# Two weight chunks a slice with alternating operations in the first tile of a windowed-attention and PReLU-FFN kernel

## The chip, the cores and the metric

One core of one Trainium2 chip runs the kernel. The metric is the device time in microseconds (us) of one execution; lower is better. Before the change three runs took 962.49, 964.57 and 964.89 us (median 964.57).

## The reference

Attention with a window (heads 0 to 3: the last 32 keys; heads 4 to 7: every fourth of the last 128 keys), and then a feed-forward layer with a PReLU on its output:

```python
B, H, S, D = 8, 8, 576, 64
scores = scale * np.matmul(q, k.transpose(0, 1, 3, 2))
scores = np.where(masks[None], scores, -1e9)
attn = np.exp(scores - scores.max(-1, keepdims=True))
attn = attn / (attn.sum(-1, keepdims=True) + 1e-9)
x = np.matmul(attn, v).astype(np.float32).transpose(0, 2, 1, 3).reshape(B * S, H * D)  # 4608 x 512
h = x @ w_in                                         # float64 weights, 512 x 2048
g = np.maximum(h, 0.0) + alpha * np.minimum(h, 0.0)
out = (g @ w_out).astype(np.float32)                 # float64 weights, 2048 x 512
```

The weights and alpha come as float64, q, k and v as float32.

## The kernel before

**Attention.** The eight heads of a batch are four pairs, and `Pair(b, c)` handles one pair. Its steps: `load_qk`, `load_v` (DMA), `scores` (72 small matmuls into two PSUM tiles), `maxima` (VectorE: twelve masked reductions of 64 columns, six for each of the two PSUM tiles), `exponentials(a, z)` (ScalarE, ten in all), `divisions` (VectorE, four operations), `transposes` (TensorE), `copies` (ScalarE), `values` (72 small matmuls), `highs` (ScalarE) and `lows` (VectorE). The last two split the attention's result into a high and a low part of a reduced fp32 format, which are the tile `x` of the feed-forward layer.

**Feed-forward.** Rows of x are taken in nine tiles of 512, and the 2048 hidden columns in sixteen slices of 128. A product is three matmul passes: high by high, high by low, low by high. For slice n: `ffn_h` (12 matmuls), `ffn_relu` (ScalarE: relu of -h and of h), `ffn_sum` (VectorE), `ffn_high` (ScalarE: g's high part), `ffn_low` (VectorE: g's low part), `ffn_y` (12 matmuls; the first needs the high part alone, the rest the low part too). Later tiles use `ffn_parts`, two VectorE operations, in place of relu and sum.

**Weights.** Both matrices are 32 chunks of 128 x 512 float64 numbers (512 KB each), loaded by `load_weight` in the order of the list `wq`. A `Conversion` makes two fp32 parts of a chunk: `magnitude` (ScalarE, the absolute value of the upper words), `words` (VectorE, four operations that each need the one before: clamp, shift, sign, lower bits), `high` (ScalarE) and `low` (VectorE). This is done only in the prologue (one chunk for each of five pairs) and the first tile.

**Order.** On TensorE, VectorE, ScalarE and SyncE the order is that of the code; each engine runs its own instructions strictly in that order, and waits come from the tiles' uses. Loads are issued by SyncE (SP). Tiles with tag `g` (staged chunks and g) share five buffers, and so do those with tag `m` (magnitudes and the relu's results): a load waits until an earlier tile's last reader is done. The prologue is the loop over `s`, in which pair s is normalised while pair s-1 is multiplied by v and pair s+1 is scored. In the first tile (`begin`, n below 16) the slices do weights and attention together: slices 2, 6, 10 and 14 score a pair, the slice after holds its `exponentials(3)` and the `highs` and `lows` of the pair before (`held`), the next its `divisions`, the next its `transposes` and `copies`.

Of the kernel before, what the change touches and what calls it, by code (L numbers as in the profile page):

```python
# [50 lines left out]
def tile_window_attention_prelu_ffn(  # L51
# [47 lines left out]
    class Pair:  # L99
# [36 lines left out]

        def maxima(self):

            self.nm = sml.tile([P, NR], F32, tag="nm", name=f"nm_{self.id}")
            for e in range(2):  # L140
                for g in range(NG + 2):
                    rows = slice(0, P) if g < NG else slice(e * BQ, (e + 1) * BQ)
                    r = e * NG + g if g < NG else 2 * NG + g - NG
                    kind = self.kinds[g] if g < NG else 1
                    nc.vector.tensor_tensor_reduce(  # L145
                        out=self.pr[rows, r, :], in0=self.ps[e][rows, g, :], in1=mask_sb[rows, kind, :],
                        scale=-SCALE, scalar=3.0e38, op0=ALU.add, op1=ALU.min, accum_out=self.nm[rows, r:r + 1],
                    )

        def exponentials(self, a=0, z=NR):  # L150
# [92 lines left out]
    class Conversion:  # L243
# [12 lines left out]
        def words(self):  # L256
            a, af = self.a, self.a.bitcast(F32)
            lo, hi = self.st[:, :, 0], self.st[:, :, 1]
            nc.vector.tensor_scalar(out=af, in0=af, scalar1=F64_LOW, scalar2=F64_HIGH, op0=ALU.max, op1=ALU.min)  # L259
            nc.vector.tensor_scalar(  # L260
                out=a, in0=a, scalar1=3, scalar2=0x3FFFFFFF, op0=ALU.logical_shift_left, op1=ALU.bitwise_and)
            nc.vector.scalar_tensor_tensor(  # L262
                out=a, in0=hi, scalar=0xC0000000, in1=a, op0=ALU.bitwise_and, op1=ALU.bitwise_or)
            nc.vector.scalar_tensor_tensor(  # L264
                out=a, in0=lo, scalar=29, in1=a, op0=ALU.logical_shift_right, op1=ALU.bitwise_or)

# [113 lines left out]
    for s in range(NC):  # L380
        u = pairs[s]
        if s:
            pairs[s - 1].copies()
            pairs[s - 1].values()
# [3 lines left out]
        pairs[s + 1].load_v()  # L388
        u.maxima()
        u.exponentials()  # L390
        w.words()
        load()
        if s:
            pairs[s - 1].highs()
            pairs[s - 1].lows()
        w.high()
        u.divisions()
        u.transposes()
        w.low()
# [3 lines left out]
    u.values()  # L403
    v.maxima()
    u.highs()
    v.exponentials(0, 5)
    u.lows()
    ffn_h(0, 0)
    w.words()
    load()  # L410
    w.high()
    v.exponentials(5)
    v.divisions()
# [9 lines left out]

    late, w1 = w, conversion()
    pending, held = [], None
    for n in range(NTILE * NF):
# [6 lines left out]
        if begin:  # L433

            ffn_sum(t, f)
            ffn_high(t, f)
            if late:
                late.low()
            w2 = conversion()
            if w1:  # L440
                w1.words()
                w1.high()
                load()
            if n + 1 < NF:
                ffn_relu(t, f + 1)
            ffn_low(t, f)
            if w1:
                w1.low()
            if n in behind_at:
                behind_at[n].exponentials(3)  # L450
            if held:
                held.highs()
                held.lows()
                held = None
            if divided:
                divided.divisions()
            if w2:
                w2.words()
                w2.high()
                load()  # L460
            pending.append((t, f))
# [25 lines left out]
        if scored:  # L487
            if not begin:
                scored.exponentials(5)
            scored.load_v()  # L490
        if begin:
            late, w1 = w2, conversion()
        if n + 1 == NF:
# [61 lines left out]
```

## Time and profile before

| | us |
|---|---|
| median of three runs | 964.57 |
| the profiled execution | 961.82 |
| its span on the core | 960.0 |
| TensorE matmuls busy | 906.3 (94%) |
| VectorE busy | 528.5 (55%) |
| ScalarE busy | 308.0 (32%) |

The profiled execution is 2.75 us below the median of the runs, which spread over 2.4 us. In rows of the profile PE is TensorE, DVE VectorE, ACT ScalarE, SP SyncE; a row of a timeline has the start in us from the beginning of the span, the duration in us, engine, line, operation, output and input tiles with shapes, and in brackets the engine's idle time ahead of it and who ended it. Two starts that lie less than a duration apart mean that the engine overlaps the end of one operation with the next. In rows of stages there stand, for each engine, busy us and the number of instructions, then the granted TensorE clock, the DMA share and GB/s.

### The profile page before, as it was taken

Reading aid. Unit: us, or ns where it says so; the run is one execution under the profiler, and the core shown is the slowest. Engines: PE = TensorE matmul, PEld = TensorE weight load, DVE = VectorE, ACT = ScalarE, POOL = GpSimd, SP = SyncE. Lnnn points to the kernel's source line nnn. Section 1 sums busy time; section 2 is a strip of 40 time slices with the busy share of each in tenths; the row PEclk is TensorE's granted clock in tenths of the full one; section 3 lists DMA queues with packets and bytes.
Section 4 is the critical chain, followed back from the end, with each engine's and each line's share of the span. In section 5 each row is a group of like instructions: output and inputs, shape, how many; then the busy total and the mean of one; then the engine's idle time right before and its main releaser. Section 6 shows DMA issues by size and latency. Waiting matters only on the chain.

```text
span 960.0 us, 19918 instructions
## 1 busy us (share of the span) xinstructions
PE 906.3 (94%) x8224; PEld 741.8 (77%) x8224; DVE 528.5 (55%) x1607; ACT 308.0 (32%) x1075; POOL 0.7 (0%) x6
## 2 busy tenths in 40 slices
PE   4777876999999999999999999999999999999998
PEld 4655655778888888888888888888888888888886
DVE  6798798575555554545555455455555544334342
ACT  5655555432333232322232223223322311111111
POOL 0000000000000000000000000000000000000000
PEclk9988988999999999999999999999999999999999
DMA  7544533031112111211121112111211000001001
GB/s 260 193 134 159 156 121 110 36 109 51 51 51 94 50 51 51 86 42 39 39 88 49 50 51 94 51 51 51 80 65 51 26 12 33 1 1 44 1 1 44
DMA packets 30139, 65.39 MB, mean 68 GB/s; under 512 B 2784, under 2 KB 11104, under 8 KB 30048
## 3 DMA queue, kind: packets, MB, share of 16 engines
q1 hardware_dynamic: 30048, 64.11, 19.5%
q8 instruction: 65, 1.06, 0.4%
q14 instruction: 26, 0.21, 0.1%
HBM read 54.67 MB, written 9.44 MB: 67 GB/s over the span
## 4 chain that ended last, share of the span: by engine, by line
PE 83%; DVE 9%; ACT 5%; issue 1%; DMA 1%; SPq 0%; ACTq 0%
PE y L325 39%; PE h L284 36%; PE o L191 3%; PE s L122 3%; ACT pr L153 2%; PE t L173 2%; DVE wa L262 2%; DVE wa L264 2%; DVE wa L260 1%; DMA q<-qT 1%; DVE wa L259 1%; DVE x L229 1%; ACT early L153 1%; DVE wo L271 1%; ACT x L225 1%
## 5 line engine op out<-in xcount | busy, mean ns | idle before, releaser
L325 PE MATMUL y<-g,wo 128*128 128x512 f32 x1728 | 430.6, 398 | 26.8 <-DVE g L317 15.7
L284 PE MATMUL h<-x,wi 128*128 128x512 f32 x1728 | 422.5, 393 | 0.3 <-DVE x L229 0.2
L325 PEld LDWEIGHTS y<-g,wo 128*128 128x128 f32 x1728 | 327.5, 191 | 100.7 <-DVE g L317 20.3
L284 PEld LDWEIGHTS h<-x,wi 128*128 128x128 f32 x1728 | 324.2, 189 | 70.2 <-DVE x L229 2.3
L312 ACT CAST g<-m 128x512 fp32r<-128x512 f32 x144 | 89.4, 621 | 521.1 <-DVE m L307 516.2
L306 DVE TENSOR_SCALAR m<-h,al 128x512 f32<-128x512 f32 x128 | 96.1, 751 | 263.9 <-PE h L284 263.0
L317 DVE TENSOR_TENSOR g<-m,g 128x512 fp32r<-128x512 f32 x144 | 99.2, 689 | 77.4 <-ACT g L312 77.4
L153 ACT ACTIVATE pr<-pr,nm 128x64 f32<-128x64 f32 x300 | 100.3, 337 | 43.3 <-DVE nm L145 43.3
L307 DVE SCALAR_TENSOR_TENSOR m<-h,m 128x512 f32<-128x512 f32 x128 | 88.5, 691 | 4.4
L145 DVE CUSTOM_DVE_ANT_0 pr<-s,mask_sb 128x64 f32<-128x64 f32 x360 | 56.3, 213 | 25.9 <-PE s L122 25.0
L153 ACT ACTIVATION_READ_ACCUMULATOR pr<-pr,nm 128x1 f32 x300 | 56.8, 189 | 0.0
L229 DVE TENSOR_TENSOR x<-o,x 128x288 fp32r<-128x288 f32 (+8 forms) x112 | 36.0, 385 | 29.5 <-ACT x L225 29.5
L122 PEld LDWEIGHTS s<-k,q 64*32 64x32 f32 x2304 | 28.6, 111 | 21.0 <-DMA q<-qT 6.3
L122 PE MATMUL s<-k,q 64*32 64x64 f32 x2304 | 34.0, 237 | 11.0 <-DMA q<-qT 11.0
L191 PE MATMUL o<-pt,v 64*64 64x32 f32 x2088 | 38.7, 223 | 3.7 <-DVE nm L145 3.6
L191 PEld LDWEIGHTS o<-pt,v 64*64 64x64 f32 x2088 | 35.1, 137 | 7.3 <-issue 3.9
L225 ACT CAST x<-o 128x288 fp32r<-128x288 f32 (+8 forms) x112 | 30.4, 384 | 4.8 <-PE o L191 4.8
L145 DVE DVE_READ_ACCUMULATOR2_ANT nm<- 128x1 f32 (+1 forms) x384 | 28.8, 75 | 0.0
L163 DVE TENSOR_TENSOR pr<-pr,rs 128x512 f32<-128x512 f32 (+1 forms) x60 | 26.6, 484 | 1.0
L173 PE MATMUL t<-ident,pr 128*128 128x128 f32 x150 | 22.6, 284 | 3.6 <-DVE pr L163 3.6
L173 PEld LDWEIGHTS t<-ident,pr 128*128 128x128 f32 x150 | 18.7, 145 | 8.2 <-ACT wa L254 2.2
L180 ACT COPY pt<-t 128x320 f32<-128x320 f32 x64 | 22.6, 398 | 7.2 <-PE t L173 7.0
(35 smaller groups left out, 237.0 us busy)
## 6 DMA issues: line engine op xcount, KB each, us to landing
v<-vW SPq DMA_DIRECT2D x29, 576.0 KB, 3.8
k<-kT SPq DMA_DIRECT2D x32, 288.0 KB, 4.2
q<-qT SPq DMA_DIRECT2D x32, 288.0 KB, 4.4
out<-ob SPq DMA_DIRECT2D x36, 256.0 KB, 2.3
ws<-w_in SPq DMA_DIRECT2D x16, 512.0 KB, 4.0
ws<-w_out SPq DMA_DIRECT2D x16, 512.0 KB, 3.9
early<-vW SPq DMA_DIRECT2D x3, 576.0 KB, 6.8
mask_sb<-masks SPq DMA_DIRECT2D x1, 128.0 KB, 4.4
```

The lines of the kernel that those rows point to most:

```text
L122: nc.tensor.matmul(self.ps[e][col * BQ:(col + 1) * BQ, g, :], lhsT=self.q[rows, j * BQ:(j + 1) * BQ], rhs=self.k[rows, first_key(j):first_ ...
L145: nc.vector.tensor_tensor_reduce(out=self.pr[rows, r, :], in0=self.ps[e][rows, g, :], in1=mask_sb[rows, kind, :], scale=-SCALE, scalar=3.0 ...
L153: nc.scalar.activation(out=self.pr[rows, r, :], in_=self.pr[rows, r, :], func=AF.Exp, bias=self.nm[rows, r:r + 1], scale=-1.0, accum_out=s ...
L173: nc.tensor.transpose(out=self.tp[e][:, g, :], in_=self.pr[:, r:r + 2, :].rearrange("q h k -> q (h k)"), identity=ident)
L191: nc.tensor.matmul(self.po[u][e * D:(e + 1) * D, j, :], lhsT=self.v[rows, e, j, :], rhs=pt[:, :BQ], start=True, stop=True,)
L229: nc.vector.tensor_tensor(out=lo, in0=src, in1=hi.bitcast(F32), op=ALU.subtract)
L284: nc.tensor.matmul(ps, lhsT=wi[:, a, f, c, :], rhs=x[:, c, e, :], start=(n == 0), stop=(n == 3 * NC - 1))
L306: nc.vector.tensor_scalar(out=m, in0=ps, scalar1=0.0, scalar2=al[:, f:f + 1], op0=ALU.min, op1=ALU.mult)
L307: nc.vector.scalar_tensor_tensor(out=m, in0=ps, scalar=0.0, in1=m, op0=ALU.max, op1=ALU.add)
L312: nc.scalar.copy(out=g[:, 0, :], in_=ms[t, f])
L317: nc.vector.tensor_tensor(out=g[:, 1, :], in0=ms.pop((t, f)), in1=g[:, 0, :].bitcast(F32), op=ALU.subtract)
L325: nc.tensor.matmul(ys[t][c], lhsT=wo[:, a, f, c * P:(c + 1) * P], rhs=g[:, e, :], start=(f == 0 and n == 0), stop=(f == NF - 1 and n == 2),)
```

## The change

Four things are changed, all ahead of the second tile. In the prologue the four `words` operations of a chunk stand between the maxima of the second PSUM tile, copies and values of the pair before come behind four of the ten exponentials, divisions and transposes come ahead of the `highs` and `lows` of the pair before, and `load()` stands further ahead. In the first tile a slice takes its two chunks together: their `words` alternate, half of them ahead of `ffn_low` and half behind it. The two `magnitude` steps of the next slice stand at the end of a slice, and the two `high` steps of a slice's chunks at the start of the next one. And `held.highs()` and `held.lows()` stand ahead of `exponentials(3)`. No instruction is added or removed.

```diff
--- before.py
+++ after.py
@@ -134,8 +134,9 @@
                     for e in range(2):
                         self.score(e, NG + g, e, HB * g + HB - 1)
 
-        def maxima(self):
-
+        def maxima(self, between=()):
+
+            between = list(between)
             self.nm = sml.tile([P, NR], F32, tag="nm", name=f"nm_{self.id}")
             for e in range(2):
                 for g in range(NG + 2):
@@ -146,6 +147,8 @@
                         out=self.pr[rows, r, :], in0=self.ps[e][rows, g, :], in1=mask_sb[rows, kind, :],
                         scale=-SCALE, scalar=3.0e38, op0=ALU.add, op1=ALU.min, accum_out=self.nm[rows, r:r + 1],
                     )
+                    if e and between:
+                        between.pop(0)()
 
         def exponentials(self, a=0, z=NR):
             for r in range(a, z):
@@ -256,13 +259,16 @@
         def words(self):
             a, af = self.a, self.a.bitcast(F32)
             lo, hi = self.st[:, :, 0], self.st[:, :, 1]
-            nc.vector.tensor_scalar(out=af, in0=af, scalar1=F64_LOW, scalar2=F64_HIGH, op0=ALU.max, op1=ALU.min)
-            nc.vector.tensor_scalar(
-                out=a, in0=a, scalar1=3, scalar2=0x3FFFFFFF, op0=ALU.logical_shift_left, op1=ALU.bitwise_and)
-            nc.vector.scalar_tensor_tensor(
-                out=a, in0=hi, scalar=0xC0000000, in1=a, op0=ALU.bitwise_and, op1=ALU.bitwise_or)
-            nc.vector.scalar_tensor_tensor(
-                out=a, in0=lo, scalar=29, in1=a, op0=ALU.logical_shift_right, op1=ALU.bitwise_or)
+            return [
+                lambda: nc.vector.tensor_scalar(
+                    out=af, in0=af, scalar1=F64_LOW, scalar2=F64_HIGH, op0=ALU.max, op1=ALU.min),
+                lambda: nc.vector.tensor_scalar(
+                    out=a, in0=a, scalar1=3, scalar2=0x3FFFFFFF, op0=ALU.logical_shift_left, op1=ALU.bitwise_and),
+                lambda: nc.vector.scalar_tensor_tensor(
+                    out=a, in0=hi, scalar=0xC0000000, in1=a, op0=ALU.bitwise_and, op1=ALU.bitwise_or),
+                lambda: nc.vector.scalar_tensor_tensor(
+                    out=a, in0=lo, scalar=29, in1=a, op0=ALU.logical_shift_right, op1=ALU.bitwise_or),
+            ]
 
         def high(self):
             nc.scalar.copy(out=self.dst[:, 0, :], in_=self.a.bitcast(F32))
@@ -379,6 +385,9 @@
     load()
     for s in range(NC):
         u = pairs[s]
+        u.maxima(w.words())
+        u.exponentials(0, 4)
+        load()
         if s:
             pairs[s - 1].copies()
             pairs[s - 1].values()
@@ -386,30 +395,26 @@
         if s + 2 <= NC:
             pairs[s + 2].load_qk()
         pairs[s + 1].load_v()
-        u.maxima()
-        u.exponentials()
-        w.words()
-        load()
+        u.exponentials(4)
+        u.divisions()
+        u.transposes()
         if s:
             pairs[s - 1].highs()
             pairs[s - 1].lows()
         w.high()
-        u.divisions()
-        u.transposes()
         w.low()
         w = conversion()
     u, v = pairs[NC - 1], pairs[NC]
     u.copies()
     u.values()
-    v.maxima()
+    v.maxima(w.words())
+    load()
+    v.exponentials(0, 4)
     u.highs()
-    v.exponentials(0, 5)
     u.lows()
     ffn_h(0, 0)
-    w.words()
-    load()
+    v.exponentials(4)
     w.high()
-    v.exponentials(5)
     v.divisions()
     ffn_relu(0, 0)
 
@@ -421,7 +426,8 @@
     divide_at = {n + (2 if n < NF else 1): u for n, u in score_at.items() if n >= 0}
     turn_at = {n + (3 if 0 <= n < NF else 2): u for n, u in score_at.items()}
 
-    late, w1 = w, conversion()
+    late, now = [w], [conversion(), conversion()]
+    late[0].high = lambda: None
     pending, held = [], None
     for n in range(NTILE * NF):
         t, f = divmod(n, NF)
@@ -432,32 +438,39 @@
             ffn_h(*divmod(n + 1, NF))
         if begin:
 
+
+            a = late[0] if late else None
+            z = late[1] if len(late) > 1 else None
+            words = [op for ops in zip(*(w.words() for w in now)) for op in ops]
+            if a:
+                a.high()
             ffn_sum(t, f)
             ffn_high(t, f)
-            if late:
-                late.low()
-            w2 = conversion()
-            if w1:
-                w1.words()
-                w1.high()
+            if z:
+                z.high()
+            if a:
+                a.low()
+            half = len(words) // 2
+            for op in words[:half]:
+                op()
+            ffn_low(t, f)
+            if z:
+                z.low()
+            for op in words[half:]:
+                op()
+            for _ in now:
                 load()
             if n + 1 < NF:
                 ffn_relu(t, f + 1)
-            ffn_low(t, f)
-            if w1:
-                w1.low()
-            if n in behind_at:
-                behind_at[n].exponentials(3)
             if held:
                 held.highs()
                 held.lows()
                 held = None
+            if n in behind_at:
+                behind_at[n].exponentials(3)
             if divided:
                 divided.divisions()
-            if w2:
-                w2.words()
-                w2.high()
-                load()
+            late, now = now, [w for w in (conversion(), conversion()) if w]
             pending.append((t, f))
         elif n + 1 < NTILE * NF:
             ffn_parts(*divmod(n + 1, NF))
@@ -488,8 +501,6 @@
             if not begin:
                 scored.exponentials(5)
             scored.load_v()
-        if begin:
-            late, w1 = w2, conversion()
         if n + 1 == NF:
             ffn_parts(1, 0)
             ffn_high(1, 0)
```

VectorE in slice 4, before: `wa` are the magnitudes that become words (`wa1_5` is chunk 5 of w_out), `ws` the staged chunks, `wo` and `wi` the finished weights (their row is a `low`), `m` and `g` those of slice 4, `pr` and `rs` the tiles of `divisions`.

```order
L299 SCALAR_TENSOR_TENSOR m_0_4_1047<-m_0_4_1047,nal_82,h_0_4_1021 128x512
L271 TENSOR_TENSOR wo_90<-wa1_5_1038,wo_90 128x512
L259 TENSOR_SCALAR wa0_7_1085<-wa0_7_1085 128x512
L260 TENSOR_SCALAR wa0_7_1085<-wa0_7_1085 128x512
L262 SCALAR_TENSOR_TENSOR wa0_7_1085<-ws0_7_911,wa0_7_1085 128x512
L264 SCALAR_TENSOR_TENSOR wa0_7_1085<-ws0_7_911,wa0_7_1085 128x512
L317 TENSOR_TENSOR g_0_4_1105<-m_0_4_1047,g_0_4_1105 128x512
L271 TENSOR_TENSOR wi_89<-wa0_7_1085,wi_89 128x512
L160 TENSOR_SCALAR rs_1_1_1122<-sums1_85 128x10
L161 RECIPROCAL rs_1_1_1122<-rs_1_1_1122 128x10
L163 TENSOR_TENSOR pr0_83<-pr0_83,rs_1_1_1122 128x512
L163 TENSOR_TENSOR pr0_83<-pr0_83,rs_1_1_1122 64x128
```

After, the same slice:

```order
L305 SCALAR_TENSOR_TENSOR m_0_4_1053<-m_0_4_1053,nal_82,h_0_4_1020 128x512
L277 TENSOR_TENSOR wi_89<-wa0_6_910,wi_89 128x512
L263 TENSOR_SCALAR wa0_7_1070<-wa0_7_1070 128x512
L263 TENSOR_SCALAR wa1_6_1072<-wa1_6_1072 128x512
L265 TENSOR_SCALAR wa0_7_1070<-wa0_7_1070 128x512
L265 TENSOR_SCALAR wa1_6_1072<-wa1_6_1072 128x512
L323 TENSOR_TENSOR g_0_4_1105<-m_0_4_1053,g_0_4_1105 128x512
L277 TENSOR_TENSOR wo_90<-wa1_5_912,wo_90 128x512
L267 SCALAR_TENSOR_TENSOR wa0_7_1070<-ws0_7_905,wa0_7_1070 128x512
L267 SCALAR_TENSOR_TENSOR wa1_6_1072<-ws1_6_1049,wa1_6_1072 128x512
L269 SCALAR_TENSOR_TENSOR wa0_7_1070<-ws0_7_905,wa0_7_1070 128x512
L269 SCALAR_TENSOR_TENSOR wa1_6_1072<-ws1_6_1049,wa1_6_1072 128x512
```

The second chunk's four words stood behind the divisions, each behind the one it needs; now the two chunks' words alternate, and each has one operation between it and the one it needs. The sum, both weight lows and g's low are all there, with g's low between the halves.

ScalarE from g's high part in slice 3 on, before (`x` are the high parts of x, `pr` the exponentials):

```order
L312 CAST g_0_3_1035<-m_0_3_901 128x512
L254 ACTIVATE wa1_5_1038<-ws1_5_899 128x512
L268 CAST wi_89<-wa0_6_1019 128x512
L293 ACTIVATE m_0_4_1047<-h_0_4_1021 128x512
L294 ACTIVATE h_0_4_1021<-h_0_4_1021 128x512
L153 ACTIVATE pr0_83,sums1_85<-pr0_83,nm_1_1_1001 128x64 x5
L153 ACTIVATE pr0_83,sums1_85<-pr0_83,nm_1_1_1001 64x64 x2
L225 CAST x_1_94<-o_1_0_0_963 128x288
L225 CAST x_1_94<-o_1_0_1_964 128x160
L225 CAST x_2_1059<-o_1_0_1_964 128x128
L268 CAST wo_90<-wa1_5_1038 128x512
```

After:

```order
L318 CAST g_0_3_1035<-m_0_3_907 128x512
L274 CAST wo_90<-wa1_4_860 128x512
L299 ACTIVATE m_0_4_1053<-h_0_4_1020 128x512
L300 ACTIVATE h_0_4_1020<-h_0_4_1020 128x512
L228 CAST x_1_94<-o_1_0_0_964 128x288
L228 CAST x_1_94<-o_1_0_1_965 128x160
L228 CAST x_2_1056<-o_1_0_1_965 128x128
L156 ACTIVATE pr0_83,sums1_85<-pr0_83,nm_1_1_1002 128x64 x5
L156 ACTIVATE pr0_83,sums1_85<-pr0_83,nm_1_1_1002 64x64 x2
L257 ACTIVATE wa0_7_1070<-ws0_7_905 128x512
L257 ACTIVATE wa1_6_1072<-ws1_6_1049 128x512
```

The x highs stood behind seven exponentials, and now ahead of them; both magnitudes (`wa` from `ws`) stand behind the exponentials, and the next slice's first weight high follows those.

VectorE in the prologue, the second half of pair 1's maxima and the words of chunk 1 of w_in, before:

```order
L145 ISA early_91,nm_0_1_327<-s_0_1_1_155,mask_sb_80 128x64
L145 ISA nm_0_1_327 128x1
L145 ISA early_91,nm_0_1_327<-s_0_1_1_155,mask_sb_80 32x64
L145 ISA nm_0_1_327 32x1
L145 ISA early_91,nm_0_1_327<-s_0_1_1_155,mask_sb_80 32x64
L145 ISA nm_0_1_327 32x1
L259 TENSOR_SCALAR wa0_1_240<-wa0_1_240 128x512
L260 TENSOR_SCALAR wa0_1_240<-wa0_1_240 128x512
L262 SCALAR_TENSOR_TENSOR wa0_1_240<-ws0_1_105,wa0_1_240 128x512
L264 SCALAR_TENSOR_TENSOR wa0_1_240<-ws0_1_105,wa0_1_240 128x512
```

After:

```order
L263 TENSOR_SCALAR wa0_1_240<-wa0_1_240 128x512
L146 ISA early_91,nm_0_1_242<-s_0_1_1_178,mask_sb_80 128x64
L146 ISA nm_0_1_242 128x1
L265 TENSOR_SCALAR wa0_1_240<-wa0_1_240 128x512
L146 ISA early_91,nm_0_1_242<-s_0_1_1_178,mask_sb_80 128x64
L146 ISA nm_0_1_242 128x1
L267 SCALAR_TENSOR_TENSOR wa0_1_240<-ws0_1_105,wa0_1_240 128x512
L146 ISA early_91,nm_0_1_242<-s_0_1_1_178,mask_sb_80 128x64
L146 ISA nm_0_1_242 128x1
L269 SCALAR_TENSOR_TENSOR wa0_1_240<-ws0_1_105,wa0_1_240 128x512
```

The four words stood behind all maxima; now one stands behind each of four maxima of the second tile.

## The prediction

> **What bounds the kernel now.** I read the page's chain first, then the busy time by stage, then one slice of the first tile on VectorE, then what stands still beside it.
>
> ```profile
> span 960.0 us, 19918 instructions
> PE 83%; DVE 9%; ACT 5%; issue 1%; DMA 1%; SPq 0%; ACTq 0%
> ```
>
> By stage (busy us of PE, PEld, DVE, ACT, POOL, then the granted clock):
>
> ```profile
> 48.50:168.40 119.90, 91.04 (x746) 70.08 (x747) 102.81 (x252) 64.56 (x166) 0.00 (x0) 0.89 0.41 136
> 191.00:960.00 769.00, 764.39 (x6566) 630.20 (x6564) 380.27 (x1133) 200.53 (x737) 0.00 (x0) 1.00 0.14 49
> ```
>
> After 191 us PE is busy 764.39 of 769: nothing the change touches is there, and it cannot shrink. From 48.5 to 168.4 PE has 91 us of work in 120, while VectorE has 103. That stage, slices 0 to 12 of the first tile, and the 48 us ahead of it are what the edit can shorten. A plain slice (n=5), from its `ffn_sum` to the next:
>
> ```profile
> 93.02 0.74 DVE L299 SCALAR_TENSOR_TENSOR m<-m,nal,h 128x512 f32<-128x512 f32 x1
> 93.79 0.69 DVE L271 TENSOR_TENSOR wo<-wa,wo 128x512 fp32r<-128x512 f32 x1
> 94.39 0.42 DVE L259 TENSOR_SCALAR wa<-wa 128x512 f32<-128x512 f32 x1
> 94.85 0.43 DVE L260 TENSOR_SCALAR wa<-wa 128x512 uint32<-128x512 uint32 x1
> 95.32 0.69 DVE L262 SCALAR_TENSOR_TENSOR wa<-ws,wa 128x512 uint32<-128x512 uint32 x1
> 96.04 0.69 DVE L264 SCALAR_TENSOR_TENSOR wa<-ws,wa 128x512 uint32<-128x512 uint32 x1
> 96.65 0.68 DVE L317 TENSOR_TENSOR g<-m,g 128x512 fp32r<-128x512 f32 x1
> 97.42 0.69 DVE L271 TENSOR_TENSOR wi<-wa,wi 128x512 fp32r<-128x512 f32 x1
> ...
> 100.28 0.74 DVE L299 SCALAR_TENSOR_TENSOR m<-m,nal,h 128x512 f32<-128x512 f32 x1
> ```
>
> VectorE never rests, yet 7.26 us pass for 12 operations. An operation that needs the one before it starts 0.03 after that one's end (94.39+0.42 to 94.85; 95.32+0.69 to 96.04); one that doesn't starts 0.08 before that end (96.04 to 96.65 is 0.61 for an operation of 0.69). The other slices add attention work and these rests:
>
> ```profile
> 48.54 0.73 DVE L299 SCALAR_TENSOR_TENSOR m<-m,nal,h 128x512 f32<-128x512 f32 x1
> 73.56 0.75 DVE L299 SCALAR_TENSOR_TENSOR m<-m,nal,h 128x512 f32<-128x512 f32 x1
> 84.51 0.74 DVE L299 SCALAR_TENSOR_TENSOR m<-m,nal,h 128x512 f32<-128x512 f32 x1
> 102.21 0.43 DVE L259 TENSOR_SCALAR wa<-wa 128x512 f32<-128x512 f32 x1 [0.46 <-ACT wa L254]
> 108.95 0.22 DVE L145 CUSTOM_DVE_ANT_0 pr<-s,mask_sb 128x64 f32<-128x64 f32 x1 [0.77 <-PE s L122]
> 110.89 0.75 DVE L299 SCALAR_TENSOR_TENSOR m<-m,nal,h 128x512 f32<-128x512 f32 x1
> 111.55 0.68 DVE L271 TENSOR_TENSOR wo<-wa,wo 128x512 fp32r<-128x512 f32 x1
> 118.78 0.89 DVE L229 TENSOR_TENSOR x<-o,x 128x288 fp32r<-128x288 f32 x3 [2.92 <-ACT x L225]
> 148.21 0.75 DVE L299 SCALAR_TENSOR_TENSOR m<-m,nal,h 128x512 f32<-128x512 f32 x1
> 168.38 0.74 DVE L299 SCALAR_TENSOR_TENSOR m<-m,nal,h 128x512 f32<-128x512 f32 x1
> ```
>
> The L299 rows are the sums of slices 0, 3, 4, 7, 11 and 13: each starts a slice. Slice 4, 84.51 to 93.02, is 8.51, a plain 7.26 and 1.25 for the four operations of `divisions`. The bracketed rows are the rests: 0.46 for a magnitude, 0.77 for the scores, 2.92 for x's high parts. The pattern repeats every four slices: 37.33 us from 73.56, 37.32 from 110.89.
>
> **The plain slice after.** Sum 0.66 (110.89 to 111.55, where nothing is waited for), first low 0.61, four alternating L259/L260 operations at duration less 0.08, so 2x0.34+2x0.35, g's low 0.61, second low 0.61, four L262/L264 at 0.61: 6.31, or 0.95 less. 0.69 of it are six dependent gaps, 0.26 the waits of the two lows for their ACT halves (93.02 to 93.79 is 0.77 instead of 0.66; 96.65 to 97.42 is 0.76 instead of 0.61). No row has an L259 after an unrelated L259, so the 0.69 lies between 0 and 0.69; I take all of it, since L264 with an unrelated successor is the nearest row.
>
> The Trainium skill (VectorE: DVE Perf Modes, section "The DRAIN you can't avoid") says the pipeline empties after every Vector operation whatever waits stand between, and advises cutting operations, not semaphores. By that rule the gaps would stay. The rows above, 0.73 behind a needed L262 against 0.61 behind L264, speak against it here.
>
> **ACT and the attention slices.** Starts and durations on ACT:
>
> ```profile
> 85.15 0.67 ACT L254 ACTIVATE wa<-ws 128x512 f32<-128x512 f32 x1
> 85.72 0.61 ACT L312 CAST g<-m 128x512 fp32r<-128x512 f32 x1
> 89.27 0.59 ACT L294 ACTIVATE h<-h 128x512 f32<-128x512 f32 x1
> 118.04 0.33 ACT L153 ACTIVATE pr<-pr,nm 64x64 f32<-64x64 f32 x1
> 118.37 0.72 ACT L225 CAST x<-o 128x288 fp32r<-128x288 f32 x3
> ```
>
> From start to start a magnitude (L254) is 0.57, 0.10 less than its duration; by the same overlap a cast is 0.52 (L312 here, L268 alike), a relu 0.49 and an exponential 0.33; three x highs take 0.72. In slices 3, 7 and 11, which follow the scores, the x highs stood behind seven exponentials (2.33), hence the rest of 2.92. Put ahead of them they end some 5 us into the slice, and VectorE reaches the lows at 6.31: that rest goes. What is late next: the exponentials now stand ahead of both magnitudes, and the next slice's first weight high behind them. How late that is depends on when PE delivers h for the relus that stand first:
>
> ```profile
> 67.87 2.79 PE L325 MATMUL y<-g,wo 128*128 128x512 f32 x11 [1.53 <-DVE g L317]
> 73.88 3.01 PE L284 MATMUL h<-x,wi 128*128 128x512 f32 x12
> 86.39 0.49 PE L325 MATMUL y<-g,wo 128*128 128x512 f32 x1 [3.06 <-ACT g L312]
> 88.88 5.06 PE L325 MATMUL y<-g,wo 128*128 128x512 f32 x11 [2.00 <-DVE g L317]
> 172.63 3.02 PE L325 MATMUL y<-g,wo 128*128 128x512 f32 x12
> ```
>
> After a scoring slice h ends 8.9 us after y began (67.87 to 73.88+2.9). y begins when g's low is done, 3.35 into slice 2 (0.66+0.61+1.38 and its own 0.69), and slice 2 lasts 9.05 (below), so h is there 3.25 into slice 3. From then on ACT has two relus 0.98, highs 0.72, exponentials 2.33, magnitudes 1.15, weight high 0.52; done at 8.95. Slice 3 lasts 6.31 and 0.80 for the x lows, 7.11; slice 4 wants that high 0.66 later, 7.77. A new stall of 1.2 in slices 4 and 8, and about 1.1 in 12.
>
> Four slices after: 7.11 (slice 3); 1.2+6.31+1.25 (4); 6.31 (5); 6.31+2.74 (6). The 2.74 are twelve maxima (108.95 to 110.89, 1.94) and the wait for the scores, 0.8. It stays: y starts with g's low, and from there to the maxima VectorE has 3.66 of work where it had 3.63 (96.65 to 100.28). Together 31.2 against 37.3, 6.1 less. The 0.46 for a magnitude goes, since both now run at the end of the slice before.
>
> **Weight loads.** A magnitude now follows its load by about a slice, not one and a half. The second chunk's buffer comes free with the last L264 of the slice before, so its DMA issues some 0.5 into the slice (behind the first chunk's, on SP). Magnitude and, at the slice's end, the first chunk's weight high follow on ACT in order, and the next slice's low needs that high at 6.97. The landing may take 6.97-0.5-0.57-0.52=5.4 us. Landings of the first kind of chunk in this stage, least, median and most:
>
> ```profile
> DMA to landing us min/median/max: 3.8/3.9/5.3
> ```
>
> So I cost this at nothing; cover is 0.1 us at the worst row, 1.5 at the median. SP keeps its order otherwise: `load()` only moves ahead of the k and q loads of the prologue, where SP stood waiting for scores anyway.
>
> **The prologue** (maxima of pair 1, of pair 4; copies of pair 1; the first h):
>
> ```profile
> 13.60 0.22 DVE L145 CUSTOM_DVE_ANT_0 early<-s,mask_sb 128x64 f32<-128x64 f32 x1
> 21.78 0.86 ACT L180 COPY pt<-t 128x320 f32<-128x320 f32 x2 [1.60 <-PE t L173]
> 37.16 0.21 DVE L145 CUSTOM_DVE_ANT_0 pr<-s,mask_sb 128x64 f32<-128x64 f32 x1
> 40.47 4.86 PE L284 MATMUL h<-x,wi 128*128 128x512 f32 x14
> ```
>
> The first step, up to 13.60, I leave as it is: its end is set by loads that are not moved. Three steps, one pair each, take 23.56 from there to 37.16. There VectorE ran maxima, four words, x lows, divisions and a weight low, and rested for ACT's exponentials and x highs. After, the four words stand between the second half of the maxima, and a step is ACT's row: exponentials from 0.25 after the first maximum (itself 0.22 long), 3.3 for ten, 0.75 for the copies between them (21.78, 0.86 long); then VectorE's divisions 1.25, x lows 0.8 and weight low 0.6. That is 7.0, with a seam 7.1; 7.5 for the step whose x tile comes in four pieces. 21.7 in all, a gain of 1.9. From pair 4's maxima to the first sum it was 11.38 (37.16 to 48.54). PE's first h began 3.3 behind those maxima (40.47). With the divisions ahead of x's lows the transposes, and so copies and values, are done 0.8 earlier against the maxima: h begins at 2.5, twelve matmuls take 4.2 (14 took 4.86), two relus 1.0: 7.7. ACT's own row (copies 0.75, ten exponentials 3.3, highs 1.0 for four pieces, a weight high 0.52, and 0.5 of waiting for the values) ends at 6.1, ahead of the relus; the words are done inside the maxima. Gain 3.7. Ends for the prologue's 5.6: nothing, if the copies behind four exponentials make PE late by as much, and 7.5, if the steps run by VectorE's work alone.
>
> **The sum**, against the profiled 961.82 (span 960.0, and 2.75 under the median of 964.57): prologue 5.6; slices 0 to 2, 25.02 before, 5.7 (no second low yet)+6.31+9.05 after, 4.0; slices 3 to 10, 12.2; slices 11 and 12, 20.17 against 7.56+8.67, 3.9; y of slice 13 begins 2.5 into its slice (one chunk's words are left), not 4.25 (168.38 to 172.63), 1.7. In all 27.4, after which PE is the bound as before. 964.57-27.4=937.2; I say 938, for small waits at the seams.
>
> **Rivals.** (a) The gaps stay: 0.69 in 13 slices and half of it in five prologue steps, 10.7 us: 949. (b) PE falls to half clock. The clock after the 3.06 and 2.00 of idle above:
>
> ```profile
> 88.90:94.40 5.50, 5.50 (x13) 4.34 (x14) 5.30 (x12) 2.22 (x5) 0.00 (x0) 0.50 0.37 104
> ```
>
> y took 5.06 for 2.79 there. Behind the new stall of slices 4, 8 and 12 PE rests 2.8, with one y matmul in it; 1.53 ahead of 67.87 did no harm. If the clock falls, 2.3 to 2.8 each, partly covered: 940 to 946. The Trainium skill (TensorE: Matmul & The Clock Gate, section "Why this matters for your kernels") warns of gaps above about 3 us between bursts; by it these sit at the edge. (c) Slower: weights land late. Two loads issue together, and in slices 3, 7, 11 k and q stand between. Each us of landing above 5.4 would cost up to 13; above 7.7 all is lost and more: at 8.5, 978. The worst row, 5.3, speaks against it; half-late loads give 950 to 962. (d) The prologue gains nothing: 943. (e) PE bounds the stage after all and nothing moves: its 91 us in 13 slices, half-clock parts with them, make 28 in four slices of 31.2, so this is excluded but for (b).
>
> **Chances.** My forecast, 932 to 943 with (d) at its edge and part of (b): 0.58. (a) or the dear part of (b), 943 to 953: 0.24. More than that gained, below 932: 0.06. Late loads in part, 953 to 961: 0.05. Within 0.3% (2.9 us, about what a measurement tells from no change): 0.02. Slower, (c): 0.05. The range of 932 to 953 leaves out 0.18. Faster 0.93, same 0.02, slower 0.05.
>
> **What would show it.** Right: plain slices of 6.3 with L259 to L259 at 0.34; no rest ahead of the x lows; a rest of about 1 ahead of the first low in slices 4, 8, 12; first sum near 43; y of slice 13 near 145. Wrong: ACT's magnitudes waiting for DMA in every slice, or dependent gaps that only moved.

## The result and the profile after

The changed kernel takes 938.21 us (median of four runs, 937.66 to 938.82) beside 964.32 us for the kernel before on the same chip (four runs, 962.49 to 964.89): a ratio of 0.9733, with a 95% interval of 0.9716 to 0.9749. The forecast was 938.0, in a range of 932 to 953. The profiled execution has a span of 935.9 us, 24.1 below the 960.0 of before.

From the page of the changed kernel, its span and the chain of work that ended last:

```profile
span 935.9 us, 19935 instructions
...
PE 86%; DVE 7%; ACT 4%; issue 1%; DMA 1%; SPq 0%; ACTq 0%
```

Busy time by stage (PE, PEld, DVE, ACT, POOL, then the granted clock), the first tile's slices 0 to 12 and what follows:

```profile
43.00:145.00 102.00, 88.64 (x761) 69.21 (x761) 93.59 (x252) 66.78 (x169) 0.00 (x0) 0.95 0.48 160
168.00:936.00 768.00, 763.12 (x6559) 628.77 (x6557) 378.95 (x1132) 200.31 (x736) 0.00 (x0) 1.00 0.14 48
```

The stage is 102 us long where it was 120. VectorE's share of it rose from 0.86 (102.81 of 119.90) to 0.92 (93.59 of 102.00), so VectorE still sets its pace. Behind it PE is as full as it was. The page counts 19935 instructions where it counted 19918, but as many matmuls (8224) and VectorE and ScalarE operations (1607 and 1075) as before.

A plain slice (n=5) on VectorE. With the new code the sum is L305, the weight low L277, the four word operations L263, L265, L267 and L269, g's low part L323; `x2` joins the two chunks' operations of one kind:

```profile
82.07 0.73 DVE L305 SCALAR_TENSOR_TENSOR m<-m,nal,h 128x512 f32<-128x512 f32 x1
82.72 0.68 DVE L277 TENSOR_TENSOR wi<-wa,wi 128x512 fp32r<-128x512 f32 x1
83.33 0.75 DVE L263 TENSOR_SCALAR wa<-wa 128x512 f32<-128x512 f32 x2
84.00 0.74 DVE L265 TENSOR_SCALAR wa<-wa 128x512 uint32<-128x512 uint32 x2
84.67 0.68 DVE L323 TENSOR_TENSOR g<-m,g 128x512 fp32r<-128x512 f32 x1
85.27 0.68 DVE L277 TENSOR_TENSOR wo<-wa,wo 128x512 fp32r<-128x512 f32 x1
85.87 1.28 DVE L267 SCALAR_TENSOR_TENSOR wa<-ws,wa 128x512 uint32<-128x512 uint32 x2
87.08 1.28 DVE L269 SCALAR_TENSOR_TENSOR wa<-ws,wa 128x512 uint32<-128x512 uint32 x2
88.28 0.73 DVE L305 SCALAR_TENSOR_TENSOR m<-m,nal,h 128x512 f32<-128x512 f32 x1
```

6.21 us where it was 7.26. Two L263 take 0.67 from start to next start, 0.34 each; two L267 take 1.21, 0.60 each. The 0.46 and 0.73 behind a needed predecessor are gone.

The starts of slices 0, 3, 7, 11 and 13 and every rest above 0.7 us for ScalarE in the stage (the rest in brackets):

```profile
44.37 0.75 DVE L305 SCALAR_TENSOR_TENSOR m<-m,nal,h 128x512 f32<-128x512 f32 x1 [0.90 <-ACT h L300]
57.73 0.69 DVE L277 TENSOR_TENSOR wi<-wa,wi 128x512 fp32r<-128x512 f32 x1 [0.79 <-ACT wi L274]
66.10 0.75 DVE L305 SCALAR_TENSOR_TENSOR m<-m,nal,h 128x512 f32<-128x512 f32 x1
75.24 0.69 DVE L277 TENSOR_TENSOR wi<-wa,wi 128x512 fp32r<-128x512 f32 x1 [1.39 <-ACT wi L274]
97.30 0.75 DVE L305 SCALAR_TENSOR_TENSOR m<-m,nal,h 128x512 f32<-128x512 f32 x1
106.43 0.69 DVE L277 TENSOR_TENSOR wi<-wa,wi 128x512 fp32r<-128x512 f32 x1 [1.39 <-ACT wi L274]
128.49 0.75 DVE L305 SCALAR_TENSOR_TENSOR m<-m,nal,h 128x512 f32<-128x512 f32 x1
137.95 0.69 DVE L277 TENSOR_TENSOR wi<-wa,wi 128x512 fp32r<-128x512 f32 x1 [1.25 <-ACT wi L274]
144.77 0.73 DVE L305 SCALAR_TENSOR_TENSOR m<-m,nal,h 128x512 f32<-128x512 f32 x1
```

The rest of 2.92 ahead of the x lows is gone. In its place stands one of 1.39, 1.39 and 1.25 ahead of the first weight low of slices 4, 8 and 12. Four slices take 31.20 (66.10 to 97.30), where they took 37.33. Slice 2 has a rest of its own, 0.79.

Two more views tell what late ScalarE and PE work stands behind these rests. On ScalarE in slices 3 and 4, the last relu, the two magnitudes and the weight high:

```profile
70.01 0.59 ACT L300 ACTIVATE h<-h 128x512 f32<-128x512 f32 x1
70.53 0.76 ACT L228 CAST x<-o 128x288 fp32r<-128x288 f32 x3
...
73.49 1.21 ACT L257 ACTIVATE wa<-ws 128x512 f32<-128x512 f32 x2
74.61 0.60 ACT L274 CAST wi<-wa 128x512 fp32r<-128x512 f32 x1
```

Between 70.53 and 73.49 stand the x highs and seven exponentials. ScalarE has no pause, and the weight high that VectorE waits for ends at 75.2. On PE, y of slices 4, 8, 12 and 13:

```profile
75.78 0.49 PE L331 MATMUL y<-g,wo 128*128 128x512 f32 x1 [0.84 <-ACT g L318]
77.93 3.97 PE L331 MATMUL y<-g,wo 128*128 128x512 f32 x11 [1.66 <-DVE g L323]
109.12 4.37 PE L331 MATMUL y<-g,wo 128*128 128x512 f32 x11 [1.64 <-DVE g L323]
140.64 4.37 PE L331 MATMUL y<-g,wo 128*128 128x512 f32 x11 [1.65 <-DVE g L323]
148.03 3.01 PE L331 MATMUL y<-g,wo 128*128 128x512 f32 x12
```

The eleven matmuls take 4 to 4.4 us in place of 2.79, behind rests of 0.84 and 1.66 with one matmul between them: here the clock did fall.

| term | forecast | in the two traces |
|---|---|---|
| prologue, to the first sum | 5.6 | 48.54 - 44.37 = 4.2 |
| slices 0 to 2 | 4.0 | 25.02 - 21.73 = 3.3 |
| slices 3 to 10 | 12.2 | 74.65 - 62.39 = 12.3 |
| slices 11 and 12 | 3.9 | 20.17 - 16.28 = 3.9 |
| y of slice 13 into its slice | 1.7 | 4.25 - 3.26 = 1.0 |
| from there to the end | 0 | 787.37 - 787.87 = -0.5 |
| sum | 27.4 | 24.1 |

The medians of this series differ by 26.1, two more than the two profiled executions, since that of before (961.82) lay 2.50 under the 964.32, and that of after (937.66) 0.55 under the 938.21. In the later series below, with seven to nine runs of it each, the kernel before takes 962.82 to 963.14; beside the changed kernel of the same series the gain is then 25.1 (962.97 - 937.87).

### The profile page after: what moved, and what is told of

It is laid out like the page before. It is cut to its first block, busy times and chain, and to the rows that moved or that the text cites. A ratio compares the mean times of both kernels' runs of the same rounds, so it can differ in the third digit from the quotient of the medians.

```text
span 935.9 us, 19935 instructions
## 1 busy us (share of the span) xinstructions
PE 897.8 (96%) x8224; PEld 736.0 (79%) x8224; DVE 517.6 (55%) x1607; ACT 308.9 (33%) x1075; POOL 0.7 (0%) x6
## 4 chain that ended last, share of the span: by engine, by line
PE 86%; DVE 7%; ACT 4%; issue 1%; DMA 1%; SPq 0%; ACTq 0%
PE y L331 40%; PE h L290 38%; PE o L194 4%; PE s L122 3%; ACT pr L156 2%; PE t L176 2%; DVE wa L267 1%; DVE wa L269 1%; DVE g L323 1%; DVE wa L263 1%; DVE wi L277 1%; DMA ws<-w_out 1%; DMA ws<-w_in 1%; DVE pr L146 1%; DVE x L232 1%
## 5 line engine op out<-in xcount | busy, mean ns | idle before, releaser
L331 PE MATMUL y<-g,wo 128*128 128x512 f32 x1728 | 425.5, 395 | 11.3 <-DVE g L323 8.1
L323 DVE TENSOR_TENSOR g<-m,g 128x512 fp32r<-128x512 f32 x144 | 99.2, 689 | 76.7 <-ACT g L318 76.7
L146 DVE CUSTOM_DVE_ANT_0 pr<-s,mask_sb 128x64 f32<-128x64 f32 x360 | 56.9, 213 | 25.9 <-PE s L122 25.1
L257 ACT ACTIVATE wa<-ws 128x512 f32<-128x512 f32 x32 | 20.8, 670 | 11.9 <-DMA ws<-w_in 5.7
```

What stands on the lines that cost most here:

```text
L146: nc.vector.tensor_tensor_reduce(out=self.pr[rows, r, :], in0=self.ps[e][rows, g, :], in1=mask_sb[rows, kind, :], scale=-SCALE, scalar=3.0 ...
L323: nc.vector.tensor_tensor(out=g[:, 1, :], in0=ms.pop((t, f)), in1=g[:, 0, :].bitcast(F32), op=ALU.subtract)
L331: nc.tensor.matmul(ys[t][c], lhsT=wo[:, a, f, c * P:(c + 1) * P], rhs=g[:, e, :], start=(f == 0 and n == 0), stop=(f == NF - 1 and n == 2),)
```

## The experiments

All are timed beside runs of the kernel before on the same chip; ratios are to those. "Changed kernel" is the kernel after.

**1. The two chunks' word operations in a row, not alternating.** All else stays as changed.

```diff
-            words = [op for ops in zip(*(w.words() for w in now)) for op in ops]
+            words = [op for w in now for op in w.words()]
```

> The changed kernel, but the two chunks' words no longer alternate: all four of the first chunk ahead of g's low, all four of the second behind it. Theory (the dependent gaps are what alternation saves): L263 to L265 again 0.45, L265 to L267 0.46, L267 to L269 0.73; 0.69 a slice, 9 us in 13 slices, of which the new stalls of slices 4, 8 and 12 (1.39, 1.39, 1.25) give back some 3, since the longer slice hides ACT's row: 944 us (943 to 947). Rival (VectorE empties after every operation anyway): starts as in the changed kernel, 938 us.

Measured: 947.45 us, ratio 0.9842 (0.9827 to 0.9857). VectorE in slice 6, one chunk's words and g's low:

```profile
94.94 0.42 DVE L263 TENSOR_SCALAR wa<-wa 128x512 f32<-128x512 f32 x1
95.39 0.43 DVE L265 TENSOR_SCALAR wa<-wa 128x512 uint32<-128x512 uint32 x1
95.85 0.69 DVE L267 SCALAR_TENSOR_TENSOR wa<-ws,wa 128x512 uint32<-128x512 uint32 x1
96.58 0.69 DVE L269 SCALAR_TENSOR_TENSOR wa<-ws,wa 128x512 uint32<-128x512 uint32 x1
97.19 0.69 DVE L323 TENSOR_TENSOR g<-m,g 128x512 fp32r<-128x512 f32 x1
...
112.79 0.69 DVE L277 TENSOR_TENSOR wi<-wa,wi 128x512 fp32r<-128x512 f32 x1 [0.60 <-ACT wi L274]
```

The dependent starts are back, 0.45, 0.46 and 0.73 (94.94 to 96.58), and the independent one stays at 0.61. A plain slice is 6.96, 0.75 more with the same operations. The Trainium skill (VectorE: DVE Perf Modes, section "The DRAIN you can't avoid") says that the pipe empties after every operation and that leaving out semaphores doesn't avoid it, but also that a next operation that is not held starts earlier. The rows agree with the second for an operation that needs nothing from the one before: the order alone moved 0.75 us a slice. Thirteen slices of 0.75 are 9.8, and the stalls of slices 4, 8 and 12 shrink by 0.8 each (1.39 to 0.60), which leaves 7.4; so much longer is the stage from the first sum to the sum of slice 13 in the two traces (smaller changes, in slice 2's stall and in the waits for the scores, cancel). In these two executions the rest lies ahead of slice 0: the first sum came at 46.53 instead of 44.37, for code that the edit doesn't touch. Whether that holds for all four runs the times don't show. I had expected a larger part to be hidden by the stalls, and so 944.

Alternation is thus not the whole of the first tile's gain. Four slices take 33.66 in this execution (70.03 to 103.69), 37.33 before and 31.20 after the change: of the 6.1 that a cycle gained, 2.5 is the alternation and 3.7 the other moves.

**2. x's high parts behind the exponentials again.**

```diff
+            if n in behind_at:
+                behind_at[n].exponentials(3)
             if held:
                 held.highs()
                 held.lows()
                 held = None
-            if n in behind_at:
-                behind_at[n].exponentials(3)
```

> The changed kernel, but in slices 3, 7 and 11 the x highs stand behind the seven exponentials again. The prediction's term (a rest of 2.9 returns three times): 946 to 947 us. My theory now: x's lows stand at the end of the slice, so a first x high 6.9 into it makes a rest of 0.6 only, and the stall of the next slice, which ACT's whole row sets, shrinks by as much: 938 to 939 us, the rests ahead of L232 about 0.6 and the ones ahead of L277 about 0.8.

Measured: 938.38 us, ratio 0.9747 (0.9733 to 0.9762): no difference from the change. VectorE in slices 3 and 4:

```profile
74.30 0.89 DVE L232 TENSOR_TENSOR x<-o,x 128x288 fp32r<-128x288 f32 x3 [0.82 <-ACT x L228]
...
76.28 0.69 DVE L277 TENSOR_TENSOR wi<-wa,wi 128x512 fp32r<-128x512 f32 x1 [0.44 <-ACT wi L274]
```

The rest of 1.39 is split in two, 0.82 and 0.44. ScalarE's whole row of slice 3 is what VectorE waits for, and the order within it decides only where.

**3. The same move alone, in the kernel before.** `held.highs()` and `held.lows()` go ahead of `exponentials(3)`, all else as before.

> The kernel before with one edit: in slices 3, 7 and 11 the x highs stand ahead of the seven exponentials. Theory: the rest of 2.92 ahead of x's lows shrinks to about 0.6 (h arrives 3.3 into the slice, relus and highs follow), 2.3 in three slices, 7 us: 957 us (956 to 959). Rival (ACT's row as a whole is what is waited for, so the wait moves to the next weight low): 963 to 964 us.

Measured: 957.29 us, ratio 0.9950 (0.9933 to 0.9966), 5.5 us less. VectorE in slice 3:

```profile
79.26 0.89 DVE L229 TENSOR_TENSOR x<-o,x 128x288 fp32r<-128x288 f32 x3 [0.62 <-ACT x L225]
```

2.92 became 0.62, since in that order the x lows stand in the middle of the slice. From the first sum to that of slice 13 this execution takes 113.02 (48.64 to 161.66) instead of 119.84, 6.8 less; 1.3 of that doesn't show in the median of four runs that spread over 3.5. So the move has a value of its own, 2.3 us three times in the traces, and experiment 2 shows that the new order takes this gain without it.

**4. The old prologue with the new first tile.** The prologue's code is that of before (word operations behind the exponentials, copies ahead of the maxima).

> The first tile of the changed kernel with the prologue of the kernel before (maxima, ten exponentials, words, x highs and lows, divisions in the old order). Theory (the prologue's share is the 4.2 us by which the first sum comes earlier): first sum near 48.5, 942 to 943 us. Rival (the earlier first sum is taken back by late weight loads in slices 1 and 2, where ACT waited 1.57 us for a load): 939 to 940 us.

Measured: 942.71 us, ratio 0.9794 (0.9778 to 0.9809); the first sum starts at 48.92. Beside experiment 2 of the same series, which equals the changed kernel (938.38), the new prologue is worth 4.3 us, and the first tile alone 20.1 (962.82 - 942.71). Up to 1.3 of the 4.3 may be another thing: in this execution VectorE waits 2.05 for the first weight low of slice 2, where it waits 0.79 in the changed kernel's. This run also tells what the half clock costs. PE and the granted clock in slice 4:

```profile
83.76 2.79 PE L331 MATMUL y<-g,wo 128*128 128x512 f32 x11 [1.65 <-DVE g L323]
```

```profile
76.80:87.90 11.10, 8.69 (x37) 6.64 (x36) 9.67 (x23) 8.24 (x26) 0.00 (x0) 1.00 0.50 166
```

With the same rests, 0.77 and 1.65, the clock stays full here, and so it does in slice 8 (y takes 2.80); only in slice 12 it falls (4.28). Four slices still take 31.20 (71.95 to 103.15). The half clock of the changed kernel costs its cycle of four slices nothing: VectorE sets the pace.

**5. The exponentials split.** Of the seven behind a scoring slice three stay, and four come a slice later, ahead of the divisions.

```diff
             if n in behind_at:
-                behind_at[n].exponentials(3)
+                behind_at[n].exponentials(3, 6 if n + 1 < NF else NR)
             if divided:
+                divided.exponentials(6)
                 divided.divisions()
```

> The changed kernel, with the exponentials behind a scoring slice split: slices 3, 7 and 11 run numbers 3 to 5, and 6 to 9 come in slices 4, 8 and 12 just ahead of the divisions. ACT's row of slice 3 is then four exponentials, 1.33 us, shorter. Theory (the new stall of 1.39, 1.39 and 1.25 us ahead of the first weight low is the length of ACT's row, and the half clock of y in these slices comes from PE's rest behind it): the three stalls go to 0.1 or less, y of slices 4, 8 and 12 takes 2.8 instead of 4.0 to 4.4, y of slice 13 begins some 0.7 earlier in its slice; 934 us (933 to 935). Rival (the row is not shorter, its end only moves: in slice 4 the relus wait for PE, and the exponentials behind them hold up both magnitudes): stalls of about 1 us ahead of the first low of slices 5, 9 and 13 instead, 937 to 939.

Measured: 934.74 us, ratio 0.9703 (0.9690 to 0.9716). VectorE in slice 4, then PE there:

```profile
76.30 0.74 DVE L305 SCALAR_TENSOR_TENSOR m<-m,nal,h 128x512 f32<-128x512 f32 x1
77.09 0.69 DVE L277 TENSOR_TENSOR wi<-wa,wi 128x512 fp32r<-128x512 f32 x1
...
83.92 0.73 DVE L305 SCALAR_TENSOR_TENSOR m<-m,nal,h 128x512 f32<-128x512 f32 x1
```

```profile
79.79 2.80 PE L331 MATMUL y<-g,wo 128*128 128x512 f32 x11 [1.38 <-DVE g L323]
```

The stall is gone: the first low starts 0.79 behind the sum instead of 2.12, slice 4 is 7.62 long instead of 8.95, and four slices take 29.89 (69.28 to 99.17). y runs at its full 2.8. The theory holds, and the rival, that the stall would only move to slice 5, does not.

**6. The prologue's word operations behind all twelve maxima.**

```diff
-        u.maxima(w.words())
+        u.maxima()
+        [op() for op in w.words()]
...
-    v.maxima(w.words())
+    v.maxima()
+    [op() for op in w.words()]
```

> The changed kernel, with a chunk's four word operations of the prologue behind all twelve maxima and no longer between the last six. Theory (they delay the last maxima, so the last exponentials, for which VectorE's divisions rest 0.69 us in each of three steps): rests of 0.2 to 0.4 instead of 0.69, a step 7.1 instead of 7.3 to 7.7, first sum 0.5 to 1 us earlier; 937.5 us (936.8 to 938). Rival (between the maxima they were covered by the wait for the exponentials anyway, and their four dependent gaps now stand in a row on VectorE): a step 0.3 to 0.5 longer, 939 to 940.

Measured: 937.12 us, ratio 0.9730 (0.9717 to 0.9743), beside 937.87 and 0.9740 (0.9726 to 0.9753) for the changed kernel in the same series: too near to tell apart by the times. The trace can. First the changed kernel, VectorE from pair 1's maxima to pair 2's:

```profile
13.87 0.23 DVE L146 CUSTOM_DVE_ANT_0 early<-s,mask_sb 128x64 f32<-128x64 f32 x1
...
18.37 0.17 DVE L163 TENSOR_SCALAR rs<-sums 128x10 f32<-128x10 f32 x1 [0.69 <-ACT early L156]
...
21.15 0.22 DVE L146 CUSTOM_DVE_ANT_0 pr<-s,mask_sb 128x64 f32<-128x64 f32 x1
```

Then this run:

```profile
13.65 0.23 DVE L146 CUSTOM_DVE_ANT_0 early<-s,mask_sb 128x64 f32<-128x64 f32 x1
...
17.96 0.17 DVE L163 TENSOR_SCALAR rs<-sums 128x10 f32<-128x10 f32 x1
...
20.74 0.22 DVE L146 CUSTOM_DVE_ANT_0 pr<-s,mask_sb 128x64 f32<-128x64 f32 x1
```

A step is 7.09 instead of 7.28, and the rest ahead of the divisions (L163) is gone. The three steps take 21.81 instead of 22.27. Between the maxima the words did no harm to VectorE, but they made the last maxima, and so the last two exponentials, late.

**7. Both, and the changed kernel once more.** Experiments 5 and 6 together:

> The two edits together: split exponentials in the first tile, words behind the maxima in the prologue. If both theories hold the gains add: 933.4 us (932 to 934.5). If only the first holds: 934 to 936; if only the second, 937 to 938.

Measured: 933.34 us, ratio 0.9697 (0.9684 to 0.9710), the gains of 5 and 6 together (3.1 and 0.8 against 4.5) within what the runs can tell. Only the second version of experiment 8 is as fast. The changed kernel in the same series:

> The changed kernel once more, beside the three others on the same chip, for the small differences: 938.2 us (937.5 to 939).

Measured: 937.87 us, ratio 0.9740 (0.9726 to 0.9753).

**8. The first k and q loads one slice later**, so that on SP they no longer stand between slice 0's weight loads and slice 1's first (by the order of the code the load behind them is slice 1's, not slice 0's second as the expectation has it); on the changed kernel and on version 7.

```diff
-        u = score_at.get(n + 3) or (score_at.get(2) if n == 0 else None)
+        u = score_at.get(n + 3) or (score_at.get(2) if n == 1 else None)
```

> The changed kernel, with the k and q loads of the first pair that is scored in the first tile issued at the end of slice 1 instead of slice 0, so that they no longer stand on SP between slice 0's two weight loads. Theory (slice 2's stall of 0.79 us ahead of its first weight low is that second weight load, issued 1.06 us late behind k and q and landing slowly beside them): it issues at about 50.0 instead of 51.06, the magnitude's wait for the DMA falls from 1.57 to 0.5 or less and slice 2's stall to at most 0.1, 0.7 to 0.8 us less in all: 937.3 us (936.5 to 938). Rival (the load is slow by itself, or the same wait goes to slice 3, whose loads k and q now meet, or to the scores): 938 to 939.

> The split exponentials, the words behind the maxima and the k and q loads one slice later together: 932.6 us (931.8 to 933.6) if the load theory holds, 933.3 to 934 if not.

Measured: 938.24 us, ratio 0.9745 (0.9732 to 0.9758), and 933.24 us, 0.9693 (0.9680 to 0.9706): no gain that the times show. ScalarE's magnitudes of slice 1, the changed kernel's second one first:

```profile
56.52 0.67 ACT L257 ACTIVATE wa<-ws 128x512 f32<-128x512 f32 x1 [1.57 <-DMA ws<-w_out]
```

and with the k and q loads later:

```profile
55.33 1.22 ACT L257 ACTIVATE wa<-ws 128x512 f32<-128x512 f32 x2
...
63.82 0.68 ACT L257 ACTIVATE wa<-ws 128x512 f32<-128x512 f32 x1 [2.02 <-DMA ws<-w_out]
```

The wait for the load is gone, and slice 2's stall with it: slices 0 to 2 take 20.86 (45.42 to 66.28), close to the 21.06 that were forecast, instead of 21.73. A wait of 2.02 has come to the next slice, as the rival had it, but nothing waits for it there. So the cause of the stall is shown, but its 0.9 us did not show in the median: in this execution the first sum came at 45.42, 1.05 later than in the changed kernel's, for work that no edit had touched.

The size of this stall varies. With the k and q loads between, slice 2 takes 9.58 to 9.93 in five executions with the new prologue; in that of experiment 5, whose code is the same up to there, the load came later (ScalarE waited 2.48 for it), and slice 2 took 12.37, where version 7 with the later k and q loads takes 9.04. So experiment 5's own execution holds 2.5 us of late load that its edit didn't cause.

## Why the prediction was right, point by point

**The plain slice** was forecast at 6.31 with all of the 0.69 of gaps taken; it is 6.21. That an independent L263 would start as early as an independent L267 was a choice of the nearest row, and experiment 1 gives back 0.75 when only the order is undone. Rival (a) is refuted.

**The four-slice cycle** came out at 31.20 for 31.2, but one of its steps was argued wrongly. I credited the end of the 2.92 rest to the x highs going ahead of the exponentials. Experiment 2 shows that in the new order this is worth nothing: the x lows now stand at the slice's end, by which time ScalarE's whole row decides. The sum held because that row was costed as a whole for the new stall: 1.2 was said, 1.39 came. That the cycle came out to the hundredth is luck: the plain operations were 0.1 a slice shorter than forecast, and this hid that the stall was 0.2 longer. Experiment 5 shows the length of that row to be the cause.

**Slices 0 to 2** gave 3.3 of 4.0. The term failed on "Weight loads. I cost this at nothing": slice 1's first load left SP at 51.06, behind the k and q loads that slice 0 issues at its end, its magnitude waited 1.57, and slice 2 stalled 0.79. I had named k and q between loads, but for slices 3, 7 and 11 alone. Experiment 8 confirms the place.

**The prologue** gave 4.2 of 5.6 in the two traces, 4.3 by experiment 4. Its steps were costed as ScalarE's row, with the words "inside the maxima" for nothing. Experiment 6 shows the price of that: 0.46 in three steps, and 21.81 without it, beside 21.7 forecast. The tail from pair 4's maxima to the first sum took 8.23 instead of 7.7; it varies more than this between executions (below).

**y of slice 13** gave 1.0 of 1.7. It was sized from VectorE's side; what came later was PE, still busy behind the half clock of slice 12. In experiment 5, without it, that y's first matmul starts 1.67 into the slice, the others 2.79. In the first execution of experiment 8, which has the stall of slice 12 but the full clock there, they start at 1.70 and 2.79: so it is the clock, and not the stall.

**Rival (b)**, the half clock behind the new stall, did come to pass, in all three places. Its price was wrong: I took 2.3 to 2.8 each, partly covered. In the cycle it was nothing (experiment 4), and only ahead of slice 13, where PE is about to become the bound, did it cost: y of slice 13 ends 6.27 into its slice in the changed kernel's execution and 7.53 in its second one, against 5.58 in experiment 8. **Rival (c)**, late weights, came true in slice 2 alone, but there in every execution with the k and q loads between and alternating words: 0.5 to 0.9 in five of them, 2.2 in experiment 4 and 3.3 in experiment 5, against slice 2's 9.04 without. **(d)**, a prologue that gains nothing, is excluded by experiment 4, and **(e)** by the result.

So the mechanisms were those forecast but for the x highs; the terms were 3.3 too large against the traces, of which 0.8 had been taken off for seams. That 938.0 and 938.21 lie so near is luck for the rest: the terms were read from an execution of before that was faster than its median and taken off that median, and this median was itself 1.4 to 1.8 above those of the later series.

## What to carry to other kernels

Where an engine seems full, look at the distance between starts: dependent operations in a row paid 0.46 and 0.73 where alternating ones paid 0.34 and 0.60, and interleaving two independent chains took 0.75 us of 6.96 off a slice without removing an instruction. When several operations of one engine stand between a producer and the engine that sets the pace, cost the whole row up to the one that is waited for; moving an operation within that stretch only moves the wait (experiment 2), and taking work out of it (experiments 3 and 5) removes it. A lower clock or a late load is a loss only where its engine is next in line, so ask of each who waits for it before it is priced.

## What the runs showed of the hardware that was not expected

The clock fell behind short rests: 0.8 to 1.3 us and then 1.4 to 1.65, with a single matmul between. In slices 4, 8 and 12 of six executions with that pattern y ran slow in 13 of 18 places and at full speed in 5, with the same rests. Behind a rest of 1.3 to 1.5 without another ahead of it, in the same slices of three executions with split exponentials, it never did (0 of 9).

The traces tell why. In all twelve the granted clock changes only on a grid of 3.41 us, which lies differently over the slices in each execution. Two such windows in slice 8 of the changed kernel, and then two in the same slice of experiment 8, first execution, where the rests are the same:

```profile
106.54:109.95 3.41, 1.33 (x5) 0.88 (x6) 3.41 (x8) 2.56 (x5) 0.00 (x0) 1.00 0.85 327
109.96:113.37 3.41, 3.41 (x10) 2.63 (x9) 3.34 (x9) 1.31 (x2) 0.00 (x0) 0.50 0.15 24
```

```profile
104.95:108.36 3.41, 1.88 (x8) 0.98 (x6) 2.08 (x6) 3.41 (x7) 0.00 (x0) 1.00 0.98 340
108.36:111.77 3.41, 2.52 (x11) 2.10 (x12) 3.41 (x7) 1.68 (x4) 0.00 (x0) 1.00 0.30 121
```

In the first, one window holds the whole longer rest and half of the shorter one, PE is busy for 1.33 of it, and the next has half the clock. In the second, the longer rest is shared by two windows, PE is busy for 1.88 and 2.52, and the clock stays. Between 45 and 165 us the twelve traces have 391 windows at full clock. In 24 of them PE is busy for 1.55 us or less, and half clock follows every one; in 360 it is busy for 1.80 or more, and half clock follows none; of the seven between, three. What counts is thus PE's busy time in a window, and not the length of one rest. A window at half clock was followed by another one where PE was busy for 2.70 or less in it (six times), and by full clock from 2.87 on (26 times).

The Trainium skill (TensorE: Matmul & The Clock Gate, section "What's actually happening") speaks of a free-running window of about 3.4 us, so that what happens depends on where in it the work lands. These windows agree with it, and each of the rests alone is less than half of one.

The prologue is less repeatable than the rest. The 70 small matmuls of pair 3's values took 1.25 to 2.14 us behind a rest of 1.1 to 1.9 that no other engine ended, and the first sum came between 43.92 and 46.53 in six executions whose code up to there is the same. Part of this is the clock again. The first twelve matmuls of h start 0.23 us apart or, at half clock, 0.43: in the changed kernel's execution the clock is half from 38.28 to 41.69, and five of these distances are 0.43; in the one with the first sum at 43.92 none is, and in that of experiment 8 eight are. What ends the rest stays open; all this limits what the times can tell of an edit worth less than about 1 us.
